# A planned attention and squared-ReLU kernel: GpSimd's compute ordered behind two-input DVE work, with GpSimd durations and queue slots as measured

## The chip, the cores and the metric

The kernel runs on one core of a Trainium2 chip. The metric is the device time of one execution in microseconds (us). Medians come with their range; each comparison stands beside runs of the kernel before on the same chip.

A ratio below is the mean time of one kernel's fast runs over the mean of the other's fast runs of the same rounds, so it is not quite the ratio of the medians that are quoted.

## The reference

```python
def _attn_ref(q, k, v):                       # q, k, v: (8, 12, 448, 64) float32
    scores = (1 / sqrt(64)) * q @ k.T
    attn = maximum(scores, 0) ** 2 / 448
    return attn @ v
def _moe_ref(x, w_in, w_out):                 # x: (3584, 768), w_in: (768, 2048), w_out: (2048, 768)
    h = x @ w_in
    return (maximum(h, 0) ** 2) @ w_out
# reference = _moe_ref(attention output as (3584, 768), w_in, w_out)
```

## The kernel before

The kernel is written as a list of operations with dependencies, buffers and guessed durations. A class `Plan` simulates the engines, lets each engine take the most urgent ready operation, tries sixteen pairs of rules with up to six estimates of DMA landing times, and emits the instructions in the order of the best simulation. So a changed duration can change the order everywhere.

How an engine picks, and how the planner books a two-input DVE operation (a sixth field in its alternative marks it):

```python
def pick(self, eng, now, waiting):            # waiting is sorted by due time
    for z, (_, _, op) in enumerate(waiting):
        if op.ready > now + 1e-9:             # not yet released: passed over
            continue
        for alt in op.alts:
            if alt[0] != eng:
                continue
            # ... rules for GpSimd against ACT ...
            if len(alt) == 5 and eng == "POOL" and sum(x > now for x in self.sent) > 7:
                continue                      # all DMA queue slots are taken
            if len(alt) > 5 and self.busy["POOL"] > now + 0.4 and op.due > now:
                continue                      # two-input DVE work while GpSimd is busy
            # ... free buffers ...
            return z, alt
```

```python
    # in simulate(): the planner thinks that GpSimd waits until the two-input DVE work ends
    if len(rest) > 1:
        self.busy["POOL"] = max(self.busy["POOL"], self.busy[eng])
```

The work of GpSimd (POOL) that matters here:

```python
def load_v(n, after=0.0, due=None):           # group n: a third of a batch; two DMA issues
    # ...
    vst[n] = plan.add([("POOL", 1.25, 1.25, emit, QK)], bufs=[buf], after=after, due=due), buf
# called with after = coming(n) - 6.0

def combine_w2():                             # eight subtractions of weights, GpSimd or DVE
    # ...
    plan.add([("POOL", 3.06, 3.1, ... nc.gpsimd.tensor_sub ...),
              ("DVE", 0.9, 0.98, ... nc.vector.tensor_sub ..., 0, True)], ...)

def combine(name, fn, deps, srcs, x, y):      # sums and differences of activations, DVE
    st[name] = plan.add([("DVE", 0.6, 0.68, emit, 0, True)], deps, [buf] + srcs), buf
```

GpSimd also squares part of the attention tiles, casts Q and K to fp16 before a DMA transpose (issued by SP), and copies the rest rows. A cast, then a transpose, then the scores: the transposed tile is called `qkt` in the traces.

## Time and profile before

| | before |
|---|---|
| median of 3 runs | 383.37 us (383.33 to 383.42) |
| profiled execution, span | 384.0 us, 382.0 us |
| PE, DVE, ACT, POOL busy | 97%, 70%, 71%, 50% |

The lines of its profile stand in the prediction. In them `L532` is the eviction of scores, `L541` the square on GpSimd, `L825` the combinations on DVE, `L810` the weight subtractions on DVE, `L424` the casts, `L474` the V loads, `L846` and `L632` the dense matmuls. In the changed kernel every line from there on is 14 to 17 higher (`L549`, `L558`, `L842`, `L827`, `L440`, `L489`, `L863`, `L649`; a subtraction on GpSimd is `L824`).

### The profile page before, as it was taken

How to read it: one execution, taken by the hardware profiler on the slowest of the kernel's cores; microseconds unless marked ns; L12 is line 12 of the kernel's file. 1: busy time of each engine (PE TensorE's matmuls, PEld its weight loads, DVE VectorE, ACT ScalarE, POOL GpSimd, SP SyncE). 2: the span in 40 equal slices, each digit the busy share in tenths (PEclk: the TensorE clock that was granted, in tenths of full speed). 3: DMA queues.
4: the chain of work that ended last, by engine and by line, in shares of the span. 5: the costliest groups of instructions: out<-in, count | busy, mean ns of one | idle time of the engine just before them, and what ended most of it. 6: DMA issues, size and time to landing. Idle time of an engine off the chain costs nothing.

```text
span 382.0 us, 8653 instructions
## 1 busy us (share of the span) xinstructions
PE 371.8 (97%) x3283; PEld 197.9 (52%) x3283; DVE 268.5 (70%) x464; ACT 272.0 (71%) x500; POOL 191.0 (50%) x184
## 2 busy tenths in 40 slices
PE   7799999999999999999999999999999999999995
PEld 3445565544465445544554555545555545555553
DVE  2976889687975677687996575885886768256731
ACT  4998999699877788687876786786794784244221
POOL 7987768383726665565564554664641333001000
PEclk9989999999999999999999999999999999999999
DMA  8999998987278966559369664674553002300243
GB/s 179 194 208 198 195 225 221 247 194 167 48 184 190 159 177 135 120 142 206 79 127 218 159 169 73 180 170 94 129 105 82 2 1 54 73 21 0 61 106 82
DMA packets 70216, 51.34 MB, mean 134 GB/s; under 512 B 36896, under 2 KB 70176, under 8 KB 70176
## 3 DMA queue, kind: packets, MB, share of 16 engines
q1 hardware_dynamic: 52384, 35.86, 38.2%
q0 software_dynamic: 16928, 14.09, 24.6%
q10 hardware_dynamic: 864, 0.85, 0.6%
q8 instruction: 25, 0.41, 0.4%
q14 instruction: 15, 0.12, 0.1%
HBM read 45.61 MB, written 11.01 MB: 148 GB/s over the span
## 4 chain that ended last, share of the span: by engine, by line
PE 92%; ACT 2%; DMA 2%; DVE 1%; POOL 1%; issue 1%; POOLq 0%; ACTq 0%
PE mm L632 38%; PE mm L846 31%; PE mm L505 10%; PE mm L570 8%; PE mm L781 3%; DMA g<-in_q_dram 2%; PE mm L681 2%; PE mm L444 1%; ACT comb L539 1%; DVE comb L825 1%; ACT rel L535 0%; POOL at L541 0%; DVE g L616 0%; ACT at L539 0%; PE mm L708 0%
## 5 line engine op out<-in xcount | busy, mean ns | idle before, releaser
L632 PE MATMUL mm<-xt,w 128*128 128x448 f16 (+1 forms) x768 | 149.0, 346 | 0.1
L541 POOL TENSOR_TENSOR at<-rel 128x896 f16<-128x896 f32 (+1 forms) x63 | 102.2, 1626 | 92.5 <-DVE rel L532 76.5
L616 DVE SCALAR_TENSOR_TENSOR g<-mm,g 128x448 f16<-128x448 f32 (+1 forms) x128 | 77.3, 605 | 50.4 <-ACT g L621 48.9
L632 PEld LDWEIGHTS <-w 128*128 128x128 f16 x768 | 72.3, 98 | 70.4 <-issue 11.7
L532 DVE TENSOR_SCALAR rel<-mm 128x448 f32<-128x448 f32 (+2 forms) x172 | 95.6, 596 | 15.7 <-PE mm L505 14.1
L621 ACT ACTIVATE g<-mm 128x448 f16<-128x448 f32 (+1 forms) x128 | 68.4, 539 | 47.2 <-PE mm L632 47.1
L539 ACT ACTIVATE at<-rel 128x896 f16<-128x896 f32 (+1 forms) x105 | 97.7, 948 | 1.1 <-DVE rel L532 0.6
L535 ACT ACTIVATE rel<-mm 128x448 f32<-128x448 f32 (+2 forms) x176 | 84.8, 550 | 2.9 <-PE mm L505 2.7
L846 PEld LDWEIGHTS <-comb 128*128 128x128 f16 x416 | 39.5, 98 | 30.3 <-issue 4.3
L765 ACT ACTIVATE part<-mm 128x384 f32<-128x384 f32 x45 | 22.3, 499 | 44.6 <-PE mm L846 42.3
L505 PE MATMUL mm<-qkt,qkt 64*64 64x448 f16 (+2 forms) x756 | 52.6, 340 | 1.4 <-DVE rel L532 0.3
L424 POOL CAST blk<-raw 128x896 f16<-128x896 f32 x36 | 36.5, 1024 | 23.4 <-DMA raw<-in_k_dram 11.7
L858 DVE SCALAR_TENSOR_TENSOR part<-mm,part 128x384 f32<-128x384 f32 x52 | 28.3, 554 | 24.9 <-ACT part L765 13.8
L846 PE MATMUL mm<-wt,comb 128*128 128x384 f16 x208 | 36.8, 327 | 0.2 <-DVE comb L825 0.2
L846 PE MATMUL mm<-w,comb 128*128 128x384 f16 x208 | 36.7, 327 | 0.0
L846 PEld LDWEIGHTS <-g 128*128 128x128 f16 x264 | 25.3, 98 | 19.1 <-issue 2.7
L570 PE MATMUL mm<-at,vs 64*64 64x448 f16 (+1 forms) x672 | 35.1, 344 | 0.0
L505 PEld LDWEIGHTS <-qkt 64*64 64x64 f16 x756 | 19.1, 106 | 26.2 <-issue 21.4
L474 POOL DMA_DIRECT2D vs<-in_v_dram x48 | 29.8, 631 | 4.2 <-DVE rel L532 2.0
L846 PE MATMUL mm<-w,g 128*128 128x384 f16 x176 | 31.1, 327 | 0.1
L570 PEld LDWEIGHTS <-vs 64*64 64x64 f16 x756 | 22.2, 108 | 14.7 <-issue 4.9
L747 POOL COPY rest<-g 128x1024 f16<-128x1024 f16 x8 | 8.8, 1103 | 40.6 <-DVE g L616 40.6
(61 smaller groups left out, 207.8 us busy)
## 6 DMA issues: line engine op xcount, KB each, us to landing
out_dram<-part SPq DMA_DIRECT2D x108, 96.0 KB, 2.2
raw<-in_k_dram SPq DMA_DIRECT2D x18, 448.0 KB, 4.2
raw<-in_q_dram SPq DMA_DIRECT2D x18, 448.0 KB, 5.0
vs<-in_v_dram POOLq DMA_DIRECT2D x48, 112.0 KB, 4.3
w<-in_moe_w_in_dram POOLq DMA_DIRECT2D x4, 768.0 KB, 11.8
w<-in_moe_w_out_dram POOLq DMA_DIRECT2D x4, 768.0 KB, 13.5
g<-in_k_dram POOLq DMA_DIRECT2D x4, 224.0 KB, 11.4
g<-in_q_dram POOLq DMA_DIRECT2D x4, 224.0 KB, 9.9
```

Source lines behind the costliest of these rows:

```text
L424: return lambda: fn(blk.tile.rearrange("p t (f d) -> p f t d", f=2), tile_of().rearrange("p f (t d) -> p f t d", d=D))
L474: nc.gpsimd.dma_start(out=buf.tile[64 * r:64 * r + 64], in_=src[:, u, hs])
L505: nc.tensor.matmul(sp[e].tile[64 * c:64 * c + 64, c0:c0 + w].rearrange("p (t c) -> p t c", c=TP), lhsT=kT[r, t, 64 * e:64 * e + 64], rhs=q ...
L532: dve(width, lambda e=e: nc.vector.tensor_scalar(out=rel()[:, e], in0=sp[e].tile[:, 0:width], scalar1=0.0, scalar2=SK, op0=ALU.max, op1=AL ...
L535: act(width, lambda e=e: nc.scalar.activation(out=rel()[:, e], in_=sp[e].tile[:, 0:width], func=AF.Relu, scale=SK))],
L539: act(n, lambda: nc.scalar.activation(out=dst(), in_=rel(), func=AF.Square)),
L541: lambda: nc.gpsimd.tensor_mul(dst(), rel(), rel()))],
L570: nc.tensor.matmul(banks[f].tile[64 * e:64 * e + 64, c0:c0 + w], lhsT=vs[r, e ^ c, t * D:(t + 1) * D], rhs=a[r, e, :], start=(t == 0), sto ...
L616: nc.vector.scalar_tensor_tensor(out=dst, in0=src, scalar=0.0, in1=dst, op0=ALU.is_gt, op1=ALU.mult)
L621: nc.scalar.activation(out=dst, in_=src, func=AF.Square)
L632: nc.tensor.matmul(bank.tile[:, c0:c0 + w], lhsT=w1[f // 4][:, m, f % 4 * P:(f % 4 + 1) * P], rhs=xts[b].tile[:, m, cols], start=(m == 0), ...
L846: nc.tensor.matmul(buf.tile[:, 0:HALF], lhsT=lhs()[:, j, :], rhs=w[:, j, :], start=(first and j == 0), stop=(j == NH - 1), skip_group_chec ...
```

## The change

The intent: the planner assumes that GpSimd stays off the shared SBUF port while a two-input DVE operation runs, but nothing made the chip keep to that. Now the first GpSimd compute instruction after such an operation gets a real wait on it. With it come a measured duration for GpSimd's squares, and V loads planned as two issues that each take a queue slot.

```diff
-        for emit in self.order:
-            emit()
+        alone = None
+        for emit, op in self.order:
+            got = emit()
+            if op is None:
+                continue
+            if len(op.way) > 5:
+                alone = got
+            elif alone is not None and op.engine == "POOL" and not op.size:
+                self.behind(got, alone)
+                alone = None
...
-  self.sent += [op.end + (0.8 if op.end > 15.0 else 0.0)] * (2 if op.size == 458752 and took > 1.0 else 1)
+  self.sent.append(op.end + (0.8 if op.end > 15.0 else 0.3))
...
+    def behind(later, first):
+        tc.add_manual_dep(later.ins, first.ins.name, mybir.DependencyInfo(
+            mybir.DependencyClass.Sync, mybir.DependencyReason.ANTI), reason="shared port")
...
-        vst[n] = plan.add([("POOL", 1.25, 1.25, emit, QK)], bufs=[buf], after=after, due=due), buf
+        vst[n] = [plan.add([("POOL", 0.62, 0.62, emit(r), QK // 2)], bufs=[buf], after=after,
+                           due=due) for r in range(2)], buf
...
-            ("POOL", 0.0018 * n + 0.05, 0.0018 * n + 0.08,
+            ("POOL", 0.13 + 0.00172 * n, 0.19 + 0.00172 * n,
```

The cut parts only return the emitted instruction and pass lists on.

More of the change, by code (lines that the diff above doesn't have):

```diff
@@ L205, in simulate @@
                         busy, took = busy + wait, took + wait
-                    op.engine, op.start = eng, begin
+                    op.engine, op.start, op.way = eng, begin, alt
                     op.end = begin + took
@@ L219, in simulate @@
                             b.tile, b.slot = slot[2], slot[1]
-                    self.order.append(emit)
+                    self.order.append((emit, op))
                     heapq.heappush(events, self.busy[eng])
@@ L259, in fill @@
             slot = min(free)
-            self.order.append(lambda: self.filler(slot[2]))
+            self.order.append((lambda: self.filler(slot[2]), None))
             self.pools["mm"].remove(slot)
@@ L348 @@
     plan.cold = 6.6
+    def behind(later, first):
+        tc.add_manual_dep(
+            later.ins, first.ins.name, mybir.DependencyInfo(
+                mybir.DependencyClass.Sync, mybir.DependencyReason.ANTI), reason="shared port")
+    plan.behind = behind
     def act(n, emit):
@@ L469, in load_v, with emit @@
         src = v[b].rearrange("(u x) (p t) d -> p u x (t d)", x=4, t=TJ)
-        def emit():
-            for r in range(2):
-                hs = slice(1, 3) if r else slice(0, 4, 3)
-                nc.gpsimd.dma_start(out=buf.tile[64 * r:64 * r + 64], in_=src[:, u, hs])
-        vst[n] = plan.add([("POOL", 1.25, 1.25, emit, QK)], bufs=[buf], after=after, due=due), buf
+        def emit(r):
+            hs = slice(1, 3) if r else slice(0, 4, 3)
+            return lambda: nc.gpsimd.dma_start(
+                out=buf.tile[64 * r:64 * r + 64], in_=src[:, u, hs])
+        vst[n] = [plan.add([("POOL", 0.62, 0.62, emit(r), QK // 2)], bufs=[buf], after=after,
+                           due=due) for r in range(2)], buf
     def load_w1(i, after, due=None):
@@ L576, in av @@
         before = av_ops.get(n, [])[-1:] + (av_ops[n - 1][-1:] if joint else [])
-        op = plan.pe(max(0.1, 0.000437 * w) * len(ts), emit, [z[0] for z in used] + [vst[n][0]] + before,
+        op = plan.pe(max(0.1, 0.000437 * w) * len(ts), emit, [z[0] for z in used] + vst[n][0] + before,
                      [z[1] for z in used] + [vst[n][1]] + banks, "tile", at)
@@ L746, in emit @@
             def emit(i=i, b=b):
-                nc.gpsimd.tensor_copy(buf.tile[:, :, 64 * i:64 * i + 64],
-                                      gts[b].tile[:, :, 3 * P:S])
+                return nc.gpsimd.tensor_copy(buf.tile[:, :, 64 * i:64 * i + 64],
+                                             gts[b].tile[:, :, 3 * P:S])
             ops.append(plan.add([("POOL", 1.55, 1.6, emit)], g_ops[b], [buf, gts[b]]))
@@ L824, in emit @@
             def emit():
-                fn(buf.tile, x(), y())
+                return fn(buf.tile, x(), y())
             st[name] = plan.add([("DVE", 0.6, 0.68, emit, 0, True)], deps, [buf] + srcs), buf
```

## The prediction

> **What bounds the kernel now.** I read the page first (busy shares, then the slices), then the chain that ended last, PE's waits, and last the instructions that the change is about. The page:
>
> ```profile
> PE 371.8 (97%) x3283; PEld 197.9 (52%) x3283; DVE 268.5 (70%) x464; ACT 272.0 (71%) x500; POOL 191.0 (50%) x184
> PE   7799999999999999999999999999999999999995
> PE 92%; ACT 2%; DMA 2%; DVE 1%; POOL 1%; issue 1%; POOLq 0%; ACTq 0%
> ```
>
> PE is busy for 97% of the span, is not full only in the first two slices and the last, and carries 92% of the chain. Busy matmul time alone can flatter PE, so I checked the rate: the chain has a piece of 96 dense 448-column matmuls in 18.17 us, 189 ns each, and one of 144 matmuls of 384 columns in 23.59 us, 164 ns each. These rates are those of the whole run: PE does not idle between its matmuls, so it is bound by its own work. In 60 to 350 us the list of PE's waits is empty; over the whole run it is this:
>
> ```profile
> PE mm L570 <- ACT comb L539: 1.3, 2, 0.7
> PE mm L988 <- DVE part L985: 1.2, 1, 1.2
> PE mm L444 <- DVE blk L409: 1.1, 1, 1.1
> PE mm L570 <- issue: 0.4, 1, 0.4
> PE mm L505 <- DVE rel L532: 0.3, 2, 0.2
> ```
>
> The columns are microseconds in total, times, longest. Small numbers: some 5 us, nearly all in the start. The stretches say where:
>
> ```profile
> 10.00:20.00 10.00, 7.62 (x213) 5.07 (x213) 9.12 (x22) 9.89 (x16) 9.46 (x13) 0.95 1.22 196
> 20.00:30.00 10.00, 9.74 (x114) 4.73 (x110) 7.45 (x17) 9.48 (x21) 8.75 (x9) 0.87 1.24 206
> 350.00:360.00 10.00, 9.84 (x61) 5.74 (x60) 8.76 (x15) 2.50 (x5) 1.56 (x1) 1.00 0.09 21
> ```
>
> After the length the columns are PE, PEld, DVE, ACT, POOL, granted clock, DMA share, GB/s. From 10 to 20 us PE has 2.4 us of holes while ACT (9.89) and POOL (9.46) are full; there the chain runs over ACT. So the whole gain within reach is: about 2.3 us before 10 us (the first loads, not touched), 2.4 + 0.3 us until 30 us, under 1 us from there to 60, and 0.2 to 0.3 us at 354 us. A gain of 2% (7.7 us) would need nearly all of PE's idle time, first loads included.
>
> **What the Trainium skill says.** "SBUF — State Buffer", Who interferes with whom: a DVE instruction with two SBUF inputs contends with a GpSimd instruction that reads SBUF; the pair is an exclusive lock for the whole instruction, and whichever started first keeps it. The trace agrees:
>
> ```profile
> L825 DVE TENSOR_TENSOR comb<-comb,g x11: 678/681/2376, 103.8 to 360.3; 128x1024 f16<-128x1024 f16 x11
> 185.16 2.38 DVE L825 TENSOR_TENSOR comb<-comb,g 128x1024 f16<-128x1024 f16 x1
> 185.15 1.83 POOL L424 CAST blk<-raw 128x896 f16<-128x896 f32 x2
> ```
>
> Alone the instruction takes 678 ns; with a cast that started 0.01 us earlier it takes 2376, two casts long. "GPSIMD Engine Reference", Elementwise side-by-side, gives 4497 ns for a two-input operation of 2048 fp32 elements, 2.2 ns per element. The trace has 1686 ns for 896 and 1263 ns for 640, so the slope is 423/256 = 1.65 ns per element and the fixed part about 0.2 us; the trace decides. "TensorE: Matmul & The Clock Gate", Part 1, has the clock fall to one half after an idle window of about 3.4 us. Here it was granted at 0.50 around 20 to 22 us, after the sparse stretch, although PE was never idle for so long at once; I keep it as a risk.
>
> **The change, part by part.** (1) The waits. In the built order 8 of the 36 casts on GpSimd gain a wait on a DVE semaphore that they did not have; each is worth at most one DVE operation, 0.68 us, on an engine that is 50% busy. In return the DVE stops being caught. What it lost before: for the combinations, 18 x (818 - 678) + 11 x (1027 - 678) + 11 x (817 - 678) + 4 x (890 - 678) ns = 2.5 + 3.8 + 1.5 + 0.8 = 8.7 us, and for the weight combinations 2 x (1372 - 944) + 2 x (1114 - 944) ns = 1.2 us. Sum 9.9 us of DVE, of which I expect most back. But nothing of it lies on PE's path between 60 and 350 us. It counts once, in the tail:
>
> ```profile
> 351.42 1.56 POOL L747 COPY rest<-g 128x1024 f16<-128x1024 f16 x1 [30.82 <-DVE g L616]
> 352.00 1.52 DVE L825 TENSOR_TENSOR comb<-g,g 128x1024 f16<-128x1024 f16 x1
> 353.45 0.68 DVE L825 TENSOR_TENSOR comb<-comb,g 128x1024 f16<-128x1024 f16 x1
> 354.18 1.47 PE L846 MATMUL mm<-wt,comb 128*128 128x384 f16 x8 [0.16 <-DVE comb L825]
> ```
>
> The copy starts first and the second combination takes 1523 ns instead of 678, so the third ends 0.84 us late, at 354.13. The previous eight matmuls began at 352.56, so PE would have been free at 352.56 + 8 x 0.163 = 353.86 and lost 0.32 us. With the copy behind the third combination that one ends near 353.3, before PE needs it: minus 0.3 us. The copy (1.04 us when alone) then runs from 353.3 to about 354.4, and its first reader began at 355.12 before, so nothing new waits.
>
> (2) The re-planning. The new GpSimd duration differs little: for 896 elements 0.13 + 0.00172 x 896 = 1.67 us against 0.0018 x 896 + 0.05 = 1.66; for 640, 1.23 against 1.20. The split V load and the queue slots change when GpSimd issues loads. Together they reorder the start: the PE order is the same until row 365, in the middle of the first scores. Two more filler matmuls stand in PE's stream (10 instead of 8); a filler is placed only where the plan sees PE idle, and they are 0.11 us apart in the trace, so I read + 0.2 us. Against it, ACT, the full engine of 10 to 30 us, has two 512-column evictions less (2 x 604 ns), one 1024-element copy less (1042 ns), and a 640-column copy and a 320-column eviction more (692 + 453 ns), plus one 128-column eviction of some 0.3 us: about 0.8 us less. I give half of that away as not on the chain and the rest as the uncertainty of moved loads: net 0.
>
> (3) The weight combinations. Two of the eight go from DVE (944 ns) to GpSimd, by the slope above 0.2 + 1536 x 1.65 = 2.7 us each, an estimate from trace rows. They stand before casts of later Q and K, around 60 to 75 us, in a stretch where GpSimd waited 3.84 us for a load. The first product with combined weights starts at 102 us, so the sums are in time, but casts behind them can arrive 1 to 2 us later and then the transposes and scores. I put + 0.2 us on it. (4) From 80 to 350 us squares, evictions and copies change places by ones and threes (three squares from GpSimd to ACT, three evictions and two output copies from ACT to DVE), with no PE wait there: 0.
>
> Sum: -0.3 + 0.2 + 0 + 0.2 = + 0.1 us: 383.4, rounded down from 383.47 because the plan now matches the trace better where GpSimd and DVE meet.
>
> **Rivals.** (a) The start gets better: V, Q and K arrive as planned, the holes of 10 to 20 us close by a third and the half clock near 20 us (six 512-column matmuls at about 400 instead of 216 ns, some 0.7 us) goes: 382.0 to 382.4. For it: ACT has less to do. Against: the extra fillers. (b) The start gets worse: a late V load or eviction moves more holes there, or casts behind the weight combinations starve scores near 75 us: 384.3 to 385.5. For it: GpSimd is 90% full until 30 us and a load issue there waits behind its compute. (c) The new waits hold up GpSimd, so squares come late and PSUM banks free late. Against: GpSimd's squares sat idle for 76.5 us in waits for their own evictions, 11 attention tiles buffer them. It would need chains of 0.68 us waits; + 0.2 us at most. (d) The DVE time given back (9.9 us) speeds up the steady state. Against: PE has no wait there; 0.
>
> **Range and chances.** Every mechanism seen is below 1 us, and (a) and (b) are the widest, about -1.3 and + 2. Range 382.2 to 384.9. Faster by over 2% would need 375.7, below what PE's idle time allows short of a perfect start: 0.01. Slower by over 2% (391.0) needs a stall of 7.6 us that no wait in the trace suggests: 0.02. Within 2%: 0.97.
>
> **What would show it.** Combinations at 0.68 us nearly everywhere, sum of excess under 3 us instead of 9.9; the second combination of the tail under 0.75 us and no PE wait at 354 us; PE's waits still empty from 90 to 350 us; two subtractions on GpSimd of about 2.7 us near 60 and 75 us; PE's holes of 10 to 30 us within 1 us of now. I am wrong if PE shows waits beyond 60 us, if the half clock lasts longer or vanishes, or if the subtractions take much longer than 2.7 us and scores wait for their transposes.

## The result, and the profile after

| | before | changed |
|---|---|---|
| median | 383.35 us (383.1 to 383.42, 4 runs) | 385.26 us (384.51 to 385.81, 4 runs) |
| span of the profiled execution | 382.0 us | 382.7 us |

The ratio is 1.005 (95% interval 1.0032 to 1.0068): slower by half a per cent, some 1.9 us. The profiled execution was the fastest of the four.

The page of the changed kernel, lines as shown of before (busy times, PE by slices, the chain by engine):

```profile
PE 371.4 (97%) x3285; PEld 197.3 (52%) x3285; DVE 263.6 (69%) x468; ACT 271.3 (71%) x497; POOL 188.3 (49%) x183
PE   8899999989999999999999999999999999999994
PE 87%; DMA 7%; issue 2%; POOL 2%; DVE 1%; ACT 0%; SPq 0%; POOLq 0%; DVEq 0%
```

DVE is 4.9 us less busy; the combinations alone shed 5.1 us of waiting for the port, as counted below. But PE has a new hole in the ninth slice, and DMA has risen from 2% to 7% of the chain: 3% of that is a weight load at the start, 2% the transposed tile `qkt`. The changed kernel's waits of PE, and its stretches (after the length: PE, PEld, DVE, ACT, POOL, granted clock, DMA share, GB/s):

```profile
PE mm L522 <- DMA qkt<-blk: 1.1, 1, 1.1
```

```profile
10.00:20.00 10.00, 8.03 (x207) 5.34 (x202) 8.95 (x19) 9.96 (x18) 9.97 (x12) 0.83 1.25 204
20.00:30.00 10.00, 9.41 (x126) 4.79 (x125) 8.12 (x18) 10.00 (x23) 8.44 (x9) 1.00 1.24 206
70.00:80.00 10.00, 8.75 (x72) 3.78 (x70) 6.37 (x13) 8.97 (x17) 9.99 (x10) 1.00 1.24 216
```

The wait is the only one of PE between 60 and 350 us, where before there was none. PE lost 1.25 us in the stretch from 70 to 80. The start is not worse: from 10 to 30 us PE was busy 17.4 us both before and after. In the tail, from 350 to 360 us, PE is busy throughout.

The tail of the changed kernel in order of time (start, length, engine, line, tiles):

```profile
352.14 0.68 DVE L842 TENSOR_TENSOR comb<-g,g 128x1024 f16<-128x1024 f16 x1
352.75 0.68 DVE L842 TENSOR_TENSOR comb<-comb,g 128x1024 f16<-128x1024 f16 x1
353.49 1.04 POOL L764 COPY rest<-g 128x1024 f16<-128x1024 f16 x1 [35.38 <-DVE comb L842]
```

The copy now stands behind the third combination, the second takes 0.68 us instead of 1.52, and PE no longer waits there: the gain of 0.3 us is as predicted.

Where the new wait came from shows in GpSimd's own order of time. First the kernel before:

```profile
57.90 1.26 POOL L474 DMA_DIRECT2D vs<-in_v_dram  x2
59.13 4.18 POOL L424 CAST blk<-raw 128x896 f16<-128x896 f32 x3
64.25 1.19 POOL L474 DMA_DIRECT2D vs<-in_v_dram  x2
```

Then the changed kernel:

```profile
58.10 3.10 POOL L824 TENSOR_TENSOR wt<-w,w 128x1536 f16<-128x1536 f16 x1 [1.31 <-DVE wt L827]
61.15 1.81 POOL L440 CAST blk<-raw 128x896 f16<-128x896 f32 x2
67.09 1.81 POOL L440 CAST blk<-raw 128x896 f16<-128x896 f32 x2 [4.13 <-issue]
68.84 2.45 POOL L489 DMA_DIRECT2D vs<-in_v_dram  x4
```

Before, the two V loads of the seventh group went out at 57.9 us and those of the eighth at 64.25. In the changed kernel a weight subtraction took that place, the casts came next, and all four V loads went out together at 68.84 us, beside two loads of Q and K and two transposes. The chain of the changed kernel then has this piece:

```profile
69.42 8.13 DMA qkt<-blk
```

A transposed tile that needs about 3 us from issue to landing when little else is on its way needed 8.13 us, and PE waited for it.

The idle time of 4.13 us before the second pair of casts is one of the new waits. In the built order the first of these two casts waits for the last of four weight subtractions in a row on DVE, which ended at 66.96 us:

```profile
65.14 1.82 DVE L827 TENSOR_TENSOR wt<-wt,w 128x1536 f16<-128x1536 f16 x2
```

Without the waits, in the same order, that cast ran straight behind the first two (three casts in a row from 60.16 us). The wait hardly delayed its transpose, because SP, which issues the transposes, came to it at 67.90 us and issued it at 68.05; but the V loads stand behind these casts, so the wait helps to hold them.

Why did the planner put the subtraction first? I followed its choice in the last planning pass. The V load has a release time, 58.5 us on the planner's clock. In the plan of before GpSimd became free just after it, in the changed plan 0.16 us before it. A free engine takes the most urgent operation that is *ready*, so it took a subtraction that nobody needs for a long time and that holds it for 3.1 us; by then the casts were more urgent than the V load. Nothing in the change aimed at this: any edit that moves GpSimd's free moment by 0.2 us can flip it. These are the planner's bookings, not times of the chip; what they cost is tested below.

### The profile page after: what moved, and what is told of

Same layout as the page of the kernel before. It is cut to its first block, busy times and chain, and to the rows that moved or that the text cites. A ratio compares the mean times of both kernels' runs of the same rounds, so it can differ in the third digit from the quotient of the medians.

```text
span 382.7 us, 8671 instructions
## 1 busy us (share of the span) xinstructions
PE 371.4 (97%) x3285; PEld 197.3 (52%) x3285; DVE 263.6 (69%) x468; ACT 271.3 (71%) x497; POOL 188.3 (49%) x183
## 4 chain that ended last, share of the span: by engine, by line
PE 87%; DMA 7%; issue 2%; POOL 2%; DVE 1%; ACT 0%; SPq 0%; POOLq 0%; DVEq 0%
PE mm L649 36%; PE mm L863 32%; PE mm L522 9%; PE mm L587 8%; DMA w<-in_moe_w_in_dram 3%; DMA qkt<-blk 2%; DMA g<-in_q_dram 2%; PE mm L698 1%; PE mm L460 1%; PE mm L798 1%; POOL blk L440 0%; PE mm L725 0%; DVE rel L549 0%; POOL at L558 0%; ACT rel L552 0%
## 5 line engine op out<-in xcount | busy, mean ns | idle before, releaser
L558 POOL TENSOR_TENSOR at<-rel 128x896 f16<-128x896 f32 (+1 forms) x60 | 96.7, 1616 | 83.5 <-DVE rel L549 65.8
L549 DVE TENSOR_SCALAR rel<-mm 128x448 f32<-128x448 f32 (+3 forms) x175 | 97.6, 599 | 17.7 <-PE mm L522 15.2
L556 ACT ACTIVATE at<-rel 128x896 f16<-128x896 f32 (+1 forms) x108 | 99.6, 947 | 1.4 <-DVE rel L549 0.9
L552 ACT ACTIVATE rel<-mm 128x448 f32<-128x448 f32 (+2 forms) x173 | 83.2, 544 | 5.3 <-PE mm L522 5.3
L440 POOL CAST blk<-raw 128x896 f16<-128x896 f32 x36 | 33.7, 947 | 32.9 <-DMA raw<-in_k_dram 14.3
```

The source lines that it names most:

```text
L440: return lambda: fn(blk.tile.rearrange("p t (f d) -> p f t d", f=2), tile_of().rearrange("p f (t d) -> p f t d", d=D))
L549: dve(width, lambda e=e: nc.vector.tensor_scalar(out=rel()[:, e], in0=sp[e].tile[:, 0:width], scalar1=0.0, scalar2=SK, op0=ALU.max, op1=AL ...
L552: act(width, lambda e=e: nc.scalar.activation(out=rel()[:, e], in_=sp[e].tile[:, 0:width], func=AF.Relu, scale=SK))],
L556: act(n, lambda: nc.scalar.activation(out=dst(), in_=rel(), func=AF.Square)),
L558: lambda: nc.gpsimd.tensor_mul(dst(), rel(), rel()))],
```

## The experiments

Two ways in which the change could cost time were open at first: **theory A**, the re-planned order around 58 to 80 us costs it; **theory B**, the new waits hold GpSimd up. Theory C blames the re-ordered start and theory D the split loads and slots through the start. Twelve runs were made (two of them the changed kernel unaltered), each of five rounds and a profiled run, on three chips; the kernel before had medians of 383.37, 382.75 and 383.23 us in the three. All outputs were correct.

| kernel | median us | ratio to before | 95% interval |
|---|---|---|---|
| changed, without its waits | 389.22 | 1.0152 | 1.0121 to 1.0183 |
| before, with the waits alone | 383.67 | 0.9994 | 0.9968 to 1.0019 |
| before, V load planned 0.3 us later | 384.92 | 1.0038 | 1.0018 to 1.0058 |
| changed, V load planned 0.3 us earlier | 382.68 | 0.9994 | 0.9967 to 1.0020 |
| changed, again | 386.74 | 1.0107 | 1.0074 to 1.0140 |
| changed, old V load and slot count | 386.73 | 1.0127 | 1.0090 to 1.0165 |
| changed, old square duration | 391.33 | 1.0219 | 1.0182 to 1.0255 |
| changed, V earlier, without waits | 386.04 | 1.0082 | 1.0066 to 1.0099 |
| changed, V loads after 76 us | 383.83 | 1.0012 | 0.9993 to 1.0030 |
| changed, no subtraction on GpSimd | 383.53 | 1.0013 | 0.9988 to 1.0037 |
| changed, both halves of V at 58 us | 383.05 | 0.9995 | 0.9975 to 1.0015 |
| changed, a third time | 384.70 | 1.0043 | 1.0022 to 1.0064 |

### The changed kernel without its waits

```diff
             elif alone is not None and op.engine == "POOL" and not op.size:
-                self.behind(got, alone)
+                pass
                 alone = None
```

The waits are no data dependency, so this is free of races, and the order of the instructions was the same on every engine.

> The changed kernel without its new waits; the order of all instructions is the same. Theory A (the re-planned order costs the time: a weight subtraction stands before the load of V for the seventh group on GpSimd, the transposed K or Q lands late and PE waits 1.1 us near 78 us): 385.0 to 385.8, ratio to before 1.004 to 1.006, and the tail wait of 0.3 us is back, so perhaps 0.3 us slower than the changed kernel. Theory B (the waits behind two-input DVE work hold GpSimd up and cost the time): 383.2 to 383.8, ratio 1.000 to 1.001.

Measured: ratio 1.0152, median 389.22 us. Theory B is refuted as the cause of the loss: without the waits the kernel is slower, not faster. How much slower is less sure, because the changed kernel stood at 1.0043, 1.0050 and 1.0107 in the others, so the waits are worth some 2 to 4 us here. Theory A's number was missed too, because it took the waits to be worth 0.3 us. PE's waits from 100 to 340 us in this run, and the place of one of them:

```profile
PE mm L863 <- DVE comb L842: 2.3, 3, 1.2
PE mm L522 <- DVE rel L549: 1.3, 1, 1.3
```

```profile
148.68 2.06 DVE L842 TENSOR_TENSOR comb<-comb,g 128x1024 f16<-128x1024 f16 x1
149.14 1.05 POOL L764 COPY rest<-g 128x1024 f16<-128x1024 f16 x1
150.80 1.47 PE L863 MATMUL mm<-wt,comb 128*128 128x384 f16 x8 [0.86 <-DVE comb L842]
```

The combination needs 0.68 us alone and took 2.06, and the matmuls that read it were next in PE's order. In the order of before such collisions never made PE wait between 60 and 350 us; in the new order four did: three made PE wait for the combination itself, one for an eviction behind two stretched combinations. The excess over 0.68 us, summed over the 52 combinations, is 8.6 us before, 10.9 us here and 3.5 us in the changed kernel. So the sum hardly differs between the two orders without waits; what differs is which collision has PE behind it.

### The kernel before with the waits alone

The loop of the diff and `behind` were put into the kernel before; durations, V loads and slots stayed, and so did the order of every engine.

> The kernel before, in its own order, with the new waits alone. Theory A: minus 0.3 us from the tail, 382.9 to 383.3, ratio 0.998 to 1.000, the second combination near 352 us at about 0.68 us. Theory B: 384.5 to 385.5, ratio 1.003 to 1.006, with PE waits that were not there.

Measured: ratio 0.9994, interval 0.9968 to 1.0019, median 383.67 us, above the range for the time. No loss, as theory A says. The gain of 0.3 us is smaller than this interval, so the time alone does not show it; the trace does. DVE's second combination of the tail with the waits:

```profile
351.90 0.68 DVE L841 TENSOR_TENSOR comb<-g,g 128x1024 f16<-128x1024 f16 x1
```

### The fault planted in the kernel before

```diff
+        for op in self.ops:
+            if op.last is not None:
+                op.last()
         once(*best[1:])
...
+        if n == 6:
+            op = vst[n][0]
+            op.last = lambda: setattr(op, "after", op.after + 0.3)
```

Only the last pass is changed, with rules and landing times already chosen, so everything before 58 us stays.

> The kernel before, with the plan's release of the V load of the seventh group 0.3 us later in the last planning pass alone, so that GpSimd takes a weight subtraction first as it does in the changed kernel; everything before 58 us is as before. Theory A: a PE wait of about 1 us for a transposed tile near 77 to 81 us, 384.2 to 385.2, ratio 1.002 to 1.005. Theory C (the re-ordered start before 58 us costs the time): no change, 383.2 to 383.6.

Measured: ratio 1.0038, median 384.92 us: slower, in the predicted range, without any of the change. GpSimd's order of time:

```profile
57.34 3.10 POOL L814 TENSOR_TENSOR wt<-w,w 128x1536 f16<-128x1536 f16 x1
63.75 1.26 POOL L478 DMA_DIRECT2D vs<-in_v_dram  x2
```

From 60 to 350 us PE has two waits of 0.5 us, both for evictions. The place of the waits was missed: none is for a transposed tile; the V loads of the seventh group came out at 63.75 us here, and only those of the eighth at 69.21. The subtraction does flip, and it costs time by moving other work, but this run does not reproduce the wait of the changed kernel. It says that a flip at 58 us alone is worth 0.7 to 2.2 us (its interval); it doesn't say through which wait.

### The changed kernel with the V load 0.3 us earlier

```diff
+        if n == 6:
+            for op in vst[n][0]:
+                op.last = lambda op=op: setattr(op, "after", op.after - 0.3)
```

> The changed kernel with that V load released 0.3 us earlier in the last planning pass alone, so that its first half goes out before the subtraction; everything before 58 us is as in the changed kernel. Theory A: the PE wait near 78 us goes, 383.6 to 384.4, ratio 1.000 to 1.003. Theory C: stays at 385.0 to 385.6, ratio 1.004 to 1.006.

Measured: ratio 0.9994, median 382.68 us, even below the range of theory A. PE's list of waits from 60 to 350 us is empty again. So the loss lies after 58 us, and theory C is refuted: this kernel has the re-ordered start of the changed one, and loses nothing. Only one of the four V loads moved, to 57.16 us; the other three still stand together near 69 us, which matters below:

```profile
68.99 1.83 POOL L493 DMA_DIRECT2D vs<-in_v_dram  x3
```

### The changed kernel again

> The changed kernel once more, unaltered, as the measure for the other three on this chip: ratio to before 1.003 to 1.007, a PE wait of 0.5 to 2 us near 78 us for a transposed tile, no other PE wait between 90 and 350 us.

Measured: median 386.74 us, ratio 1.0107, runs from 385.03 to 389.04 us: outside the range, and far more spread than the kernel before on this chip (382.08 to 383.93). This time the profiled execution was the slowest of its runs. From 60 to 350 us PE has one wait, 3.5 us for the transposed tile. A piece of its chain, and two stretches:

```profile
69.86 10.43 DMA qkt<-blk
```

```profile
75.00:80.00 5.00, 1.89 (x12) 0.62 (x10) 2.68 (x5) 4.91 (x8) 4.60 (x6) 0.93 1.48 182
80.00:83.00 3.00, 2.57 (x10) 0.90 (x10) 1.69 (x3) 0.00 (x0) 1.17 (x2) 0.50 1.02 329
```

The same tile took 10.43 us, PE waited 3.5 us, and then the clock was granted at one half, from about 79.3 to 86.1 us. In the chain of this run the 6 dense matmuls after it took 2.35 us, 392 ns each instead of 189. The clock gate that the prediction kept as a risk ("TensorE: Matmul & The Clock Gate", Part 1: half the clock after about 3.4 us of idleness) agrees with this: the wait of 1.1 us in the first profile had left the clock at 1.00, the one of 3.5 us did not. The three profiles of the changed kernel (waits of 1.1, 3.5 and 1.0 us at 384.51, 389.04 and 383.22 us) point to this one transfer as the source of its spread; a single profile, the fastest of its runs, had shown the small end of it.

### Each half of the re-planning undone

One run took back the V load and the slot count, the other the duration of the squares; both keep the waits.

```diff
-        vst[n] = [plan.add([("POOL", 0.62, 0.62, emit(r), QK // 2)], ...) for r in range(2)], buf
+        vst[n] = plan.add([("POOL", 1.25, 1.25, emit, QK)], bufs=[buf], after=after, due=due), buf
```

> The changed kernel with the V loads unsplit and the old count of queue slots: the waits and the new GpSimd duration remain. Its built order has three weight subtractions on GpSimd between 56 and 80 us instead of two, yet the V load goes out near 63 us. Theory A (the place of the V load and the subtractions sets the loss): 383.5 to 385.0, ratio 1.000 to 1.004. Theory D (split loads and queue slots are what costs, through the start): 383.0 to 383.5, ratio 0.999 to 1.001, with the start as before.

Measured: median 386.73 us, ratio 1.0127; both ranges missed, and theory D with them. Its trace has a PE wait of 1.6 us for a transposed tile and one of 0.6 us for an eviction; the V loads of the seventh group went out at 64.32 us, those of the eighth at 69.79. The two waits are less than the loss, and no run follows the rest.

```diff
-            ("POOL", 0.13 + 0.00172 * n, 0.19 + 0.00172 * n,
+            ("POOL", 0.0018 * n + 0.05, 0.0018 * n + 0.08,
```

> The changed kernel with the old GpSimd duration for the squares: the waits, the split V loads and the queue slots remain. Its built order has one weight subtraction on GpSimd, at the end of the stretch, and no subtraction before the V load. Theory A: no PE wait near 78 us, 382.4 to 383.6, ratio 0.997 to 1.001. Theory D: 384.5 to 385.5, ratio 1.003 to 1.006.

Measured: median 391.33 us, ratio 1.0219, the slowest of all, where theory A had promised no loss. Its order has no subtraction before the V load. GpSimd's order of time, and PE's waits:

```profile
58.53 3.32 POOL L558 TENSOR_TENSOR at<-rel 128x896 f16<-128x896 f32 x2 [2.72 <-DVE rel L549]
70.67 1.27 POOL L489 DMA_DIRECT2D vs<-in_v_dram  x2
```

```profile
PE mm L522 <- DMA qkt<-blk: 4.9, 1, 4.9
```

Here squares held GpSimd at 58 us, two V loads went out at 70.67 us all the same and a third at 73.07, and the transposed tile came 4.9 us late. So the subtraction as such is not the cause. That splits theory A in two: **A1**, whatever holds GpSimd up delays the casts and so the tile; **A2**, the V loads that are pushed to 69 to 73 us crowd the DMA engines while the tile is on its way. It also shows that neither half of the re-planning is the safe one: each gives another order, and each order had two or more V loads near 70 us.

### The V load earlier, without the waits

The two edits above together.

> The changed kernel with the seventh V load first and without the waits. If collisions on the shared port are worth some 4 us in any re-planned order: 386.5 to 388.0, ratio 1.008 to 1.013, with PE waits for combinations between 140 and 210 us. If the 4 us without the waits were due to the late V load as well: 382.8 to 384.0, ratio 0.999 to 1.002.

Measured: ratio 1.0082, in the first range, median 386.04 us, just below it; both far above the second. With the V load in time and the waits taken away, PE waits 1.7 us for one combination, at 149.7 us; the sum over all combinations is 13.2 us above 0.68 each. So the waits are worth some 3 us in this re-planned order too (0.9994 against 1.0082, measured on two chips); the listed wait is about half of that, and the rest is not followed here.

### The V loads moved out of the crowd

```diff
+        if n in (6, 7):
+            for op in vst[n][0]:
+                op.last = lambda op=op: setattr(op, "after", 76.0)
```

Subtraction, casts and transposes stay where the changed kernel has them, and SP's order is the same until 97 us; the four V loads go later, and on GpSimd a copy and squares move into their place.

> The changed kernel with the V loads of the seventh and eighth group moved out of the crowded stretch, to after 76 us in the last planning pass; GpSimd still does the weight subtraction before the four casts, and the casts and transposes stand as in the changed kernel. Theory A2 (the four V loads at 69 to 72 us crowd the DMA engines while the transposed tile of the eighth group is on its way): the tile lands in about 5 us instead of 8 to 10, no PE wait near 78 us, ratio to before 0.997 to 1.001, 381.8 to 383.6. Theory A1 (the subtraction holds up the casts, whatever the V loads do): the PE wait stays, ratio 1.004 to 1.011.

Measured: ratio 1.0012, interval 0.9993 to 1.0030, median 383.83 us, both a little above the ranges. PE has no wait from 60 to 350 us. GpSimd's order of time:

```profile
58.53 3.10 POOL L831 TENSOR_TENSOR wt<-w,w 128x1536 f16<-128x1536 f16 x1 [1.31 <-DVE wt L834]
67.52 1.81 POOL L444 CAST blk<-raw 128x896 f16<-128x896 f32 x2 [4.13 <-issue]
78.77 1.27 POOL L493 DMA_DIRECT2D vs<-in_v_dram  x2
```

The casts start no earlier than in the changed kernel (67.52 us against 67.09), and yet the tile is in time. This refutes A1 and supports A2. How long the two transposes between 66 and 74 us took from issue to landing, median of the two (tile, queue, operation, count, us), in the changed kernel, in its second profile, here, and in the kernel before, in this order:

```profile
qkt<-blk SPq DMA_TRANSPOSE x2, 7.1
```

```profile
qkt<-blk SPq DMA_TRANSPOSE x2, 9.0
```

```profile
qkt<-blk SPq DMA_TRANSPOSE x2, 5.8
```

```profile
qkt<-blk SPq DMA_TRANSPOSE x2, 6.2
```

The Trainium skill has the reason that fits: DMAs issued by different engines run on the same 16 DMA engines and interleave ("DMA: Bandwidth & Descriptors", Issuing engines are not separate DMA queues). The trace agrees: from 73 to 77 us, while the late tile was on its way, the queue of GpSimd's loads (q0) took this many packets, MB and share of the 16 engines' time in the changed kernel, and none with the V loads moved:

```profile
q0 software_dynamic: 576, 0.46, 79.2%
```

That is 3.2 us of all 16 engines, and the late tile itself took 8.13 us in the changed kernel.

Two runs limit the reading. In the kernel before, one transpose took 7.5 us beside a K and a Q load and stores, with no V load issued in that stretch, and PE did not wait: a long transfer costs only where PE is next to read it. And in the kernel with the V load 0.3 us earlier, three V loads stood in the crowd and PE did not wait either; there one transpose stood among them and not two, the three before it having been issued by 66.1 us. So late V loads alone do not make the wait; where it was longest they stood beside two transposes issued back to back. No run moved a transpose alone.

### No subtraction on GpSimd

```diff
+            for op in t_ops[name]:
+                op.last = lambda op=op: op.alts.pop(0)
```

> The changed kernel with no weight subtraction on GpSimd in the last planning pass; of the four V loads one goes out near 64 us and three still near 69 us. Theory A1: the PE wait goes, ratio 0.997 to 1.001. Theory A2: a wait of 0.5 to 2 us for a transposed tile near 76 to 80 us stays, ratio 1.001 to 1.006.

Measured: ratio 1.0013, interval 0.9988 to 1.0037; inconclusive between the two theories. The trace has one PE wait of 0.5 us, at 75.8 us, put down to an output store. A quarter of the V loads had left the crowd here, so a small wait fits A2, but it is no proof.

### Both halves of the V load first

The `last` of the earlier run also sets their due time to 30.0, so that the second half isn't put off behind the casts.

> The changed kernel with both halves of the seventh V load at 58 us, before the casts, and nothing else asked for; one subtraction then falls to DVE by itself. Both theories: no PE wait near 78 us; as a version that may beat both kernels 381.8 to 383.0, ratio 0.996 to 0.999, the tail without its wait.

Measured: ratio 0.9995, interval 0.9975 to 1.0015, median 383.05 us, just above both ranges: it does not beat the kernel before. No PE wait from 60 to 350 us. On the same chip the unaltered changed kernel gave this:

> The changed kernel, unaltered, as the measure on this chip: ratio to before 1.004 to 1.011, with the PE wait near 78 us of 1 to 4 us.

Measured: ratio 1.0043, median 384.70 us, with a PE wait of 1.0 us for the transposed tile in its profile, which was the fastest of its runs. Put beside each other, releasing one load 0.3 us earlier in the plan and calling it urgent, which sends it out 12 us earlier on the chip (56.60 against 68.63 us) and re-orders GpSimd behind it, is worth 0.0048 of 383.2 us, 1.8 us: the whole loss of the change on this chip. As a version, none of the twelve beats the kernel before beyond the noise; five have an interval that holds 1.

## Why the prediction was wrong

The prediction said 383.4 us, with 382.2 to 384.9; it became 385.26. Its steps:

- **What bounds the kernel** was right: PE is bound by its own work, and the losses that were followed were PE's waits, and the half clock after the long ones. A slip of no weight: six matmuls at 400 instead of 216 ns would be 1.1 us, not 0.7; the chain shows 1.92 against 1.29 us for six.
- **(1) The waits, in the tail**: right, 0.3 us in the trace, by the mechanism named. Of the 9.9 us of DVE time "most" came back: the combinations' excess fell from 8.6 to 3.5 us, a little short of the "under 3" named as a sign.
- **(1) "each is worth at most one DVE operation, 0.68 us"**: wrong. The operation that is waited for can stand behind others in DVE's order: the cast near 63 us was held 4.13 us, behind four subtractions.
- **(1) "nothing of it lies on PE's path between 60 and 350 us"**: true for the order of before and carried over to an order that did not exist when the profile was taken. Without the waits the new order has 3.6 us of listed PE waits between 100 and 340 us, and the tail's besides. The waits earned some 2 to 4 us, not 0.3, and that gain was needed to get back near where the old order stood.
- **(2) The start, net 0**: right in the sum. The kernel with the new start and the V load in time is at 0.9994; no run tests the single terms. The half clock moved, to about 15 to 18 us; its mean over 10 to 30 us stayed at 0.91.
- **(3) The weight subtractions, + 0.2 us**: this is the step that failed. Its cast and transpose part is close to what was seen: the wait was for a transposed tile, near 78 us, and a subtraction took 3.10 us against 2.7 estimated. But the casts were not what made the tile late: with the V loads alone out of the way they stood as late, and PE did not wait. The path was another one. The subtraction, with the held cast behind it, pushed the V loads from 57.9 and 64.25 us to 68.84 us, into the same microseconds as two Q and K loads and two transposes, and the tile took 8 to 10 us to land. The term measured 1.8 us, nine times what was put on it, and its wait varies from 1.0 to 3.5 us over the three profiles, with the half clock behind the long one. The order that shows the four V loads standing together was there to be read; I read the order of the subtractions and casts and not that of the loads.
- **Rival (b)** named the casts behind the subtractions near 75 us, and put 384.3 to 385.5 on it. The time fell there, partly by luck: its place was right, its mechanism half right, since the tile was late by the loads and not by the casts.
- **Rival (c)**, waits that hold GpSimd up, was rightly set aside as the sum, since the waits gain more than they cost; but one of them held GpSimd 4.13 us before the late loads, and what that one costs alone is not tested. **Rival (d)**, that the DVE time is worth nothing in the steady state, holds for the old order only.

Open: why four collisions met PE in the new order and none in the old one. The sums are alike, 10.9 and 8.6 us, so it may be chance of alignment; no run here tells it from a cause. Also open is which of the loads in the crowd weighs most on the transpose: the run that moved all four V loads doesn't say. It is open too how much of it needs the two transposes in a row.

## What to carry to other kernels

A wait that makes the chip keep to the plan's order of two engines on a shared port cost nothing measurable in the old order here and saved some 2 to 4 us in two re-planned ones; but look what stands in front of what it waits for. Judge such a wait without its re-planning, and the re-planning without it: here the re-planning alone cost 5.8 us (1.0152), and the sum of both hid that. Where a list scheduler makes the order, give long work of low urgency no chance to start just before the release of a load, and read the order of the loads in the new program before anything else: loads that bunch can be waits somewhere else. One profile of a kernel whose runs spread is a sample; profile one of its slower executions as well.

## What the Trainium skill lacked or had wrong

- "DMA: Bandwidth & Descriptors" gives an effective bandwidth of a DMA transpose, but no landing time beside loads. The runs show about 3 us with little else on its way, 7.5 us beside a Q and a K load and stores, 8.13 and 10.43 us beside four V loads and two Q and K loads.
- "TensorE: Matmul & The Clock Gate": the fall after about 3.4 us of idleness agrees with the wait of 3.5 us here. But the clock of the kernel before was also granted at 0.50 around 20 to 22 us, after a stretch from 12 to 19 us in which PE was busy 4.93 of 7.00 us and never waited more than 0.7 us at once. A sparse stretch was enough. The page tells of a kernel whose short idle gaps made the clock go to and fro, but not how sparse is too sparse.
- "SBUF — State Buffer": the exclusive lock is as the page says. No page says what a collision costs in a tuned order: nearly the same sum, 8.6 and 10.9 us, was worth 0.3 us in one order and some 2 to 4 us in another.
- "SBUF — State Buffer", Who interferes with whom, lets whoever issues first keep the port; the trace shows starts, not issues. In the kernel without waits a combination is shown to start at 148.68 us, the copy at 149.14 us, and the combination still ends 0.55 us after the copy. The spans of GpSimd are rough, and a V load was being issued there from 148.50 us, so this is an observation and no refutation.
- "GPSIMD Engine Reference" has no fp16 figure for two-input work. The subtraction of 1536 fp16 elements took 3.10 to 3.15 us, 2.0 ns per element; its 2.2 ns for fp32 is close to that, while the squares here took 1.88.
